# Three product banks instead of four: a streamed half unit of Wo kept in PSUM, and the left K and V half passes placed anew

## The chip, the cores and the metric

The kernel runs on one core of one Trainium2 chip. The metric is the time of one execution on the device in microseconds; a time given for a kernel is the median of several runs.

## The reference

The program computes `x + A(xn) + B(xn)`, where `xn` is the layer norm of `x` (2048 rows of 1024, bf16). `B` is a two-layer perceptron with a GELU (1024 to 3584 to 1024). `A` is a recurrent attention: the rows are cut into 64 segments of 32, and each segment attends to 8 memory rows and itself; the memory rows that come out are the memory of the next segment. So the 64 segments follow one another.

```python
for s in range(n_seg):                      # 64 segments
    xs = x[:, s * seg_len:(s + 1) * seg_len, :].copy()
    h = jnp.concatenate([mem, xs], axis=1)  # 8 + 32 rows
    q = jnp.einsum('btd,dhe->bhte', h, Wq)  # 32 heads of 128
    k = jnp.einsum('btd,dhe->bhte', h, Wk)
    v = jnp.einsum('btd,dhe->bhte', h, Wv)
    scores = jnp.einsum('bhqe,bhke->bhqk', q, k) * scale
    scores = jnp.where(mask[None, None], scores, -1000000000.0)
    p = _softmax(scores, axis=-1)
    o = jnp.einsum('bhqk,bhke->bhqe', p, v)
    o = jnp.einsum('bhte,hed->btd', o, Wo)
    mem = o[:, :M, :].copy()
    outs.append(o[:, M:, :])
```

## The kernel before, in words

**Two stages.** The first stage (up to about 428 us) is the layer norm and the perceptron over all rows. The second is the loop over the 64 segments (line 626), which this change is about.

**Units.** The four weight matrices of the attention are cut into 64 units of 128 partitions x 2048 bf16 (512 KB). Wk, Wq and Wv have 16 each (eight slices of the contraction, times two halves of the heads, u = 0 and 1), Wo has 16, of two heads each. SBUF holds 46 of them for good ("resident"); the other 18 are "streamed": each segment loads them anew from copies in DRAM named `Wc_...` (line 192) into a ring of six slots (`RING`, `STREAM_BUFS`). Two are special. `IN_PSUM`, the fourth of the streamed ones (a unit of Wq), is held in PSUM in two banks named `kept`, and VectorE copies it into its ring slot each segment (line 226). `HALF`, the first streamed unit of Wo, has one of its two heads resident in `half_home`; its other half (256 KB) is streamed.

**Order in a segment.** TensorE works in program order through six half passes and the output product: K0, Q0, K1, Q1, V0, V1 (eight units each), then O (16 units). After each streamed unit `unit_done` calls `start_stream`, which starts the load (SyncE's queue) or the copy (VectorE's queue) of the streamed unit six places further on; nothing else sets the order of the loads. A scheduler doesn't reorder anything: each engine executes its instructions in the order of the source.

**Banks.** A half pass accumulates in one PSUM bank that `new_acc` takes from `free_banks` (four names, `acc0` to `acc3`, in turn), and `let_go` gives it back in program order; a matmul into a bank waits until the copy out of it is done. Of the eight banks four are `acc`, one is `mixed` (scores and softmax sums in its lower half, memory rows and some of the value products in its upper half), one `beside` (masks and kept parts of q), two `kept`. The output product's bank is `psX`.

**Left rows.** Of each segment's 32 rows 24 are worked on with the 8 memory rows, as 32. The 8 rows that are "left" are gathered over a group of four segments (32 rows, `hrL`) and pass through each half pass once a group: a left half pass doubles the products of that half pass. With i4 = 0 to 3 the segment's place in its group (line 627), lines 636 to 639 say where: left K in both half passes at i4 = 0, left Q0 at 1, left Q1 at 2, left V in both at 3. The first segment does all of them. The output product takes the left rows along at i4 = 1. Up to six of a left half pass's products (of resident units) are made ahead of time at the end of the segment before (`lead_products`, line 659), while TensorE would wait for the memory rows; the bank of this left product stays taken until then.

**Attention work inside the passes.** The lists `at` (lines 856 to 892) say after which unit of a pass a step is put: `scores(0)` after Q1's first unit, `sums(0)` after its last; in V1 `scores(1)` after the first unit, `values(0, 0)`, `values(0, 1)`, `sums(1)` after units 2, 4 and 6; in O `values(1, 0)` and `values(1, 1)` after units 4 and 6. `scores(u)` fills `mixed`, ScalarE takes the exponential, VectorE applies the mask (L770). `sums(u)` sums on TensorE, ScalarE takes the logarithm and an exponential for the reciprocal (L788, L789), VectorE multiplies (L790, L792). `values(u, r)` multiplies with v and copies the result to `d_oL` (u = 0) or `b_oL` (u = 1), the inputs of the output product. Rows of K and Q are copied from PSUM by ScalarE (L693) and transposed on VectorE (L707); left ones are copied by VectorE too (`turn_kL`, `turn_qL`), and left V rows by VectorE (`left_values`, L697). `q_left` (L729) puts the left rows of q beside the segment's.

**GpSimd's queue** carries the small loads: the next rows (`load_x_rows`), the next left rows (`load_left_rows`, after K1 of a segment with i4 = 0), the residual rows (`load_res`), and the writes of the output.

Of the kernel before, what the change touches and what calls it, by code (L numbers as in the profile page):

```python
# [78 lines left out]
def kernel(  # L79
# [105 lines left out]
    for k in range(7):  # L185
# [7 lines left out]
        unit: dram.tile([P, 1024 if unit == HALF else 2048], BF16, name="Wc_" + "_".join(map(str, unit)))[:, :]  # L193
        for unit in ORDER if IS_STREAMED[unit]
    }

    def fetch(t, unit):
        w, i, u = unit
        if unit == HALF:
            h = 4 * i + 2 * u  # L200
            nc.sync.dma_start(out=half_home[:, :], in_=Wo_v[:, h, :])
            nc.sync.dma_start(out=t, in_=Wo_v[:, h + 1, :])
        elif w == "O":
            h = 4 * i + 2 * u
            nc.sync.dma_start(out=t.rearrange("p (h d) -> p h d", d=DM), in_=Wo_v[:, h:h + 2, :])
        else:
            nc.sync.dma_start(out=t, in_=W_v[w][:, i, 2048 * u:2048 * u + 2048])
# [12 lines left out]
    def start_stream():  # L220
        nonlocal started
        if started < len(streams):
            t = slab(RING[started % STREAM_BUFS])
            if streams[started] == IN_PSUM and "kept" in nxt:
                for b in range(2):
                    nc.vector.tensor_copy(out=t[:, 1024 * b:1024 * b + 1024], in_=nxt["kept"][:, b, :])  # L226
            else:
                c0 = 1024 if streams[started] == HALF else 0
                nc.sync.dma_start(out=t[:, c0:2048], in_=copies[streams[started]])
# [3 lines left out]
    nxt = {}  # L233
# [37 lines left out]
    with tc.tile_pool(name="ma", bufs=2) as ma, tc.tile_pool(name="mps", bufs=6, space=PSUM) as mps:  # L271
# [160 lines left out]
        for tg in range(4):  # L432
# [80 lines left out]
            else:  # L513


                for _ in range(STREAM_BUFS):
                    start_stream()
                fetch_resident(*(place for place in RES_PLACES if place.startswith("w1_")))
# [29 lines left out]
                fetch_resident("xt2", "xt3")  # L548

# [5 lines left out]
    with tc.tile_pool(name="late", bufs=1) as late, \  # L555
# [7 lines left out]
        free_banks = deque(f"acc{k}" for k in range(4))  # L563
# [12 lines left out]
        tr = mixed[:, 256:512].bitcast(BF16).rearrange("p (c t) -> p c t", c=4)  # L576
# [5 lines left out]
        kept = banks.tile([P, 2, 1024], BF16, name="kept")  # L582

        def keep_unit(t):

            for n in range(4):
                for k in range(4):
                    nc.tensor.transpose(tr[:, k, :], t[:, 512 * n + P * k:512 * n + P * (k + 1)], ident)
                turned = late.tile([P, 512], BF16, name="VL0").rearrange("p (k t) -> p k t", k=4)
                nc.vector.tensor_copy(out=turned, in_=tr)  # L590
                for k in range(4):
                    c0 = 512 * (n % 2) + P * k
                    nc.tensor.transpose(kept[:, n // 2, c0:c0 + P], turned[:, k, :], ident)
            nxt["kept"] = kept
# [29 lines left out]
        for t in outs:  # L624
            nc.vector.memset(t[:, :, 0:32], 0.0)
        for s in range(NSEG):
# [9 lines left out]
            left_k = i4 == 0  # L636
            left_q = [first or (i4 == 1 and more), first or (i4 == 2 and more)]
            left_v = first or (i4 == 3 and more)
# [29 lines left out]
            def half_pass(w, u, left, at):  # L668
# [10 lines left out]
                for i in range(KT):  # L679
# [4 lines left out]
                    if first and (w, i, u) == IN_PSUM:  # L684
                        keep_unit(t)
# [108 lines left out]
            def values(u, r):  # L794

                V, (prA, prB) = st["V", u], st["pr", u]
                low_bank = r == 1 or (left_v and not first)
# [41 lines left out]
            psK, psKL = half_pass("K", 0, left_k, {})  # L839
            turn_k(psK, 0)  # L840
            if left_k:
                turn_kL(psKL, 0)
            psQ, psQL = half_pass("Q", 0, left_q[0], {})
            if first:
                turn_qL(psQL, 0)
# [5 lines left out]
            psK1, psK1L = half_pass("K", 1, left_k, {})  # L851
            st["kT", 1] = nat_home
            rows_out(psK1, nat_home, nc.scalar.copy)
            if left_k and more and not first:
                load_left_rows(g + 1, nc.gpsimd)
# [4 lines left out]
            if left_k:  # L860
                at[1] = [lambda: turn_kL(psK1L, 1)]
            psQ1, psQ1L = half_pass("Q", 1, left_q[1], at)
# [7 lines left out]
            psV, psVL = half_pass("V", 0, left_v, {})  # L870
# [4 lines left out]
            if left_v and not first:  # L875
# [6 lines left out]
            psV1, psV1L = half_pass("V", 1, left_v, at)  # L882
            st["V", 1] = values_out(psV1, sp.tile([P, 512], BF16, name="v", tag="a"), nc.scalar.copy)
            if first:
# [3 lines left out]
            if first:  # L888
# [4 lines left out]
            if left_v and not first:  # L893
# [107 lines left out]
```

## Time and profile before

| what | value |
|---|---|
| median of 7 runs | 1980.27 us (1973.54 to 1989.91) |
| the profiled execution's own time | 1986.99 us |
| its span, first to last instruction | 1985.2 us |
| granted TensorE clock, mean | 0.982 |
| PE busy | 1774.6 us (89%) |
| PEld (weight loads) busy | 963.9 us (49%) |
| DVE busy | 854.7 us (43%) |
| ACT busy | 591.2 us (30%) |
| POOL busy | 287.0 us (14%) |
| DMA moved | 644.36 MB, mean 325 GB/s |

How to read it: PE is TensorE's matmuls, PEld its weight loads, DVE VectorE, ACT ScalarE, POOL GpSimd, SP SyncE, whose queue issues nearly all weight loads. The busy share of PE is not its peak: matmuls overlap, and their ends are modelled. A row of the page's groups names line, engine, operation, what it writes and reads, how often, and then busy time, mean ns of one, and the idle time of its engine ahead of it with the releaser of most of that. "issue" is time for which no releaser is seen. The line numbers are those of the kernel before.

### The profile page before, as it was taken

To read this page: it belongs to the slowest core of one execution; us is meant where nothing else is said; L and a number is where in the kernel's file an instruction comes from. 1 tells how busy PE (TensorE), PEld (TensorE's weight loads), DVE (VectorE), ACT (ScalarE), POOL (GpSimd) and SP (SyncE) were. 2 spreads that over 40 slices of the span, in tenths; PEclk is the share of its full clock that TensorE was granted. 3 is DMA by queue.
4 is the path that set the end of the run, shared out by engine and by line. 5 is a ranking of instruction groups with operands and counts; after the bars stand their busy time and mean duration, and the time that the engine had idled before them with its cause. 6 is when DMAs were issued, how large, how long until landed. Compare 5 with 4: busy or idle time off the path is not lost.

```text
span 1985.2 us, 77130 instructions
## 1 busy us (share of the span) xinstructions
PE 1774.6 (89%) x34271; PEld 963.9 (49%) x34291; DVE 854.7 (43%) x2233; ACT 591.2 (30%) x1349; POOL 287.0 (14%) x557
## 2 busy tenths in 40 slices
PE   6999999999798989898888888889888989889887
PEld 3444444445445554455454545455545455544544
DVE  6656565424343443343434333434344343444333
ACT  4433333312222222232222222222222222222222
POOL 0000000002331111111111111111111111111112
PEclk9999999999999999999999999999999999999999
DMA  9821212789999999999999999999999999999998
GB/s 328 271 52 46 53 44 52 266 304 377 380 356 379 377 382 360 359 385 375 373 373 380 386 363 368 383 364 381 361 388 368 388 377 390 376 382 381 364 354 334
DMA packets 225850, 644.36 MB, mean 325 GB/s; under 512 B 48123, under 2 KB 61739, under 8 KB 225500
## 3 DMA queue, kind: packets, MB, share of 16 engines
q1 hardware_dynamic: 207228, 619.26, 83.2%
q0 software_dynamic: 16928, 18.77, 2.9%
q8 instruction: 268, 4.39, 0.9%
q10 hardware_dynamic: 1360, 1.39, 0.2%
q14 instruction: 66, 0.54, 0.1%
HBM read 625.08 MB, written 31.26 MB: 331 GB/s over the span
## 4 chain that ended last, share of the span: by engine, by line
PE 64%; DMA 25%; issue 6%; DVE 3%; ACT 1%; POOL 1%; ACTq 0%; POOLq 0%; DVEq 0%
PE acc L650 28%; DMA u<-Wc_O 12%; PE acc L829 11%; PE ps L450 10%; DMA u<-Wc_V 9%; PE ps L498 7%; DMA u<-Wc_Q 3%; PE ps L531 2%; DMA out_dram<-res 2%; PE mixed L803 1%; DVE b_oL L707 1%; PE acc L803 1%; PE mixed L753 1%; PE pT L531 1%; DMA res<-hr_d 1%
## 5 line engine op out<-in xcount | busy, mean ns | idle before, releaser
L650 PE MATMUL acc<-u,hr 128*32 128x512 bf16 x11520 | 790.6, 382 | 32.3 <-DMA u<-Wc_V 13.5
L650 PEld LDWEIGHTS <-hr 128*32 128x32 bf16 x12288 | 350.9, 97 | 309.4 <-issue 66.2
L650 PE MATMUL acc<-u,hrL 128*32 128x512 bf16 x2880 | 263.8, 394 | 7.3 <-issue 7.2
L829 PE MATMUL acc<-u,d_oL 128*32 128x256 bf16 (+1 forms) x3330 | 187.0, 294 | 21.9 <-issue 14.1
L450 PE MATMUL ps<-u 128*128 128x512 bf16 x896 | 196.2, 382 | 2.6 <-ACT u L346 2.6
L829 PE MATMUL acc<-u,b_oL 128*32 128x256 bf16 (+1 forms) x1776 | 126.4, 302 | 55.4 <-DMA u<-Wc_O 27.7
L829 PEld LDWEIGHTS <-b_oL 128*32 128x32 bf16 (+1 forms) x3552 | 115.0, 102 | 113.9 <-issue 82.4
L498 PE MATMUL ps<-u 128*128 128x512 bf16 x657 | 146.2, 379 | 0.8
L450 PEld LDWEIGHTS <-u 128*128 128x128 bf16 x896 | 88.2, 98 | 109.3 <-issue 5.1
L829 PEld LDWEIGHTS <-d_oL 128*32 128x32 bf16 (+1 forms) x3552 | 101.4, 99 | 65.7 <-issue 40.0
L650 PEld LDWEIGHTS <-hrL 128*32 128x32 bf16 x3072 | 90.1, 98 | 66.1 <-issue 27.8
L829 PE MATMUL acc<-W_O,b_oL 128*32 128x256 bf16 (+1 forms) x1776 | 111.5, 300 | 7.5 <-issue 7.5
L879 POOL DMA_DIRECT2D res<-hr_d x64 | 35.8, 559 | 567.2 <-DVE d_oL L816 325.6
L707 DVE STREAM_TRANSPOSE kT<-kT 128x512 bf16<-128x512 bf16 x64 | 45.5, 711 | 167.0 <-ACT kT L693 167.0
L226 DVE COPY u<-kept 128x1024 bf16<-128x1024 bf16 x126 | 81.1, 686 | 79.3 <-PE acc L829 62.7
L803 PEld LDWEIGHTS <-v 32*128 32x128 bf16 x2048 | 63.6, 91 | 101.0 <-issue 76.8
L707 DVE STREAM_TRANSPOSE b_oL<-b_oL 128x512 bf16<-128x512 bf16 x128 | 90.6, 708 | 45.9 <-ACT b_oL L693 45.9
L693 ACT CAST kT<-acc 128x512 bf16<-128x512 f32 x64 | 37.4, 585 | 224.4 <-PE acc L650 224.4
L498 PEld LDWEIGHTS <-u 128*128 128x128 bf16 x672 | 65.3, 98 | 77.4 <-DVE g_u L466 0.4
L816 DVE CAST b_oL<-acc 128x160 bf16<-128x160 f32 x128 | 41.5, 324 | 139.9 <-PE acc L809 139.9
L963 POOL DMA_DIRECT2D out_dram<-res x124 | 63.4, 517 | 248.1 <-DVE res L925 247.5
L693 ACT CAST b_oL<-acc 128x512 bf16<-128x512 f32 x128 | 75.4, 589 | 79.5 <-PE acc L650 79.5
(139 smaller groups left out, 2222.5 us busy)
## 6 DMA issues: line engine op xcount, KB each, us to landing
u<-Wc_O SPq DMA_DIRECT2D x320, 512.0 KB
u<-Wc_K SPq DMA_DIRECT2D x256, 512.0 KB
u<-Wc_V SPq DMA_DIRECT2D x256, 512.0 KB
u<-Wc_Q SPq DMA_DIRECT2D x193, 512.0 KB
u<-Wc_O SPq DMA_DIRECT2D x64, 256.0 KB
u<-in_B_w_dram SPq DMA_DIRECT2D x16, 448.0 KB
u<-in_B_w_dram SPq DMA_DIRECT2D x14, 512.0 KB
u<-in_A_Wq_dram SPq DMA_DIRECT2D x12, 512.0 KB
```

The source lines that it names most:

```text
L226: nc.vector.tensor_copy(out=t[:, 1024 * b:1024 * b + 1024], in_=nxt["kept"][:, b, :])
L450: nc.tensor.matmul(ps[:, :].rearrange("p (s t) -> p s t", t=SEG), lhsT=w1_sb[fb // 14 * 8 + kt][:, (fb % 14) * P:(fb % 14 + 1) * P], rhs=x ...
L498: nc.tensor.matmul(ps[:, :], lhsT=gts[fc // 4][:, fc % 4, t * P:(t + 1) * P], rhs=w2_sb[fc // 2][:, fc % 2, cs], start=(fc == 0), stop=(fc ...
L531: nc.tensor.matmul(pss[2 * t + nb][:, :], lhsT=gts[fc // 4][:, fc % 4, t * P:(t + 1) * P], rhs=w2_sb[fc // 2][:, fc % 2, nb * 512:nb * 512 ...
L650: nc.tensor.matmul(o, lhsT=lhs[:, i, :], rhs=m, start=(i == seq[0]), stop=(i == seq[-1]), tile_position=(0, 32 * j),)
L693: cp(out=out, in_=ps.rearrange("p (h e) -> p h e", e=32))
L707: nc.vector.transpose(out=home, in_=home)
L803: nc.tensor.matmul(oV[b][:, c, :], lhsT=V[q, c * P:(c + 1) * P], rhs=prA[q, c, :], start=(c == 0), stop=False, skip_group_check=True, tile ...
L816: cp(out=outs[u][:, hs, NL * slot:NL * slot + 40], in_=oV[b])
L829: nc.tensor.matmul(acc[r:r + n // 8, 0:n], lhsT=lhs[:, 4 * (i % 4) + 2 * u + k, :], rhs=w_k[:, n * jq:n * jq + n], start=(unit == O_UNITS[ ...
L879: nc.gpsimd.dma_start(out=st["res"][:, :], in_=hr_d[s + 1, :, 256:512])
L963: nc.gpsimd.dma_start(out=out_flat[rows, 256 * j:256 * j + 256], in_=res[32 * j:32 * j + NX, :])
```

## The change

Four things change together.

1. `kept` has three banks instead of two, and `free_banks` three names instead of four. The third bank keeps the half of `HALF` that was streamed. `start_stream` copies it from PSUM into its ring slot with one VectorE instruction each segment, in place of a 256 KB load. The slot and its place in the ring stay.
2. `IN_PSUM` and `HALF` have no copy in DRAM any more. The first time `IN_PSUM` is loaded from the weights. `half_home` is loaded once by a DMA of its own, and the other half is loaded into `d_oL` at the end of the first stage, from where it goes to PSUM. `keep` fills a bank by transposing 1024 columns twice on TensorE with copies by VectorE and ScalarE between; `keep_unit` did the same for all 2048 columns with VectorE's copies alone. The zeroing of `d_oL` and `b_oL` moves behind it in the first segment.
3. The left half passes: K0 at i4 = 3 and K1 at i4 = 0 (before: both at 0), V0 at i4 = 3 and V1 at i4 = 0 (before: both at 3). The products made ahead are those of K1, Q0, Q1 and K0 (before: K0, Q0, Q1, V0). The left K0 rows, made at i4 = 3, are turned after Q1's second unit; the left V1 rows are copied at the end of V1. The next left rows are loaded after V1 of a segment with i4 = 0.
4. In `values`, the upper half of `mixed` is used for one of the two results also when the segment has a left V half pass (u = 0), as before for left V segments in both.

```diff
     def start_stream():
...
-            if streams[started] == IN_PSUM and "kept" in nxt:
-                for b in range(2):
-                    nc.vector.tensor_copy(out=t[:, 1024 * b:1024 * b + 1024], in_=nxt["kept"][:, b, :])
+            unit = streams[started]
+            if unit in kept_in:
+                for c0, bank in kept_in[unit]:
+                    nc.vector.tensor_copy(out=t[:, c0:c0 + 1024], in_=bank)
+            elif unit in copies:
+                nc.sync.dma_start(out=t[:, :], in_=copies[unit])
             else:
-                c0 = 1024 if streams[started] == HALF else 0
-                nc.sync.dma_start(out=t[:, c0:2048], in_=copies[streams[started]])
+                fetch(t[:, :], unit)
...
                 for _ in range(STREAM_BUFS):
                     start_stream()
+                h = 4 * HALF[1] + 2 * HALF[2]
+                nc.sync.dma_start(out=half_home[:, :], in_=Wo_v[:, h, :])
...
                 fetch_resident("xt2", "xt3")
+                nc.sync.dma_start(out=d_oL[:, :], in_=Wo_v[:, h + 1, :])
...
-        free_banks = deque(f"acc{k}" for k in range(4))
+        free_banks = deque(f"acc{k}" for k in range(3))
...
-        kept = banks.tile([P, 2, 1024], BF16, name="kept")
-
-        def keep_unit(t):
-
-            for n in range(4):
+        kept = banks.tile([P, 3, 1024], BF16, name="kept")
+
+        def keep(unit, c0, w, bank):
+
+            turned = [late.tile([P, 512], BF16, name=f"VL{n}").rearrange("p (k t) -> p k t", k=4) for n in range(2)]
+            for n in range(2):
                 for k in range(4):
-                    nc.tensor.transpose(tr[:, k, :], t[:, 512 * n + P * k:512 * n + P * (k + 1)], ident)
-                turned = late.tile([P, 512], BF16, name="VL0").rearrange("p (k t) -> p k t", k=4)
-                nc.vector.tensor_copy(out=turned, in_=tr)
+                    nc.tensor.transpose(trs[n][:, k, :], w[:, 512 * n + P * k:512 * n + P * (k + 1)], ident)
+                (nc.scalar.copy if n else nc.vector.tensor_copy)(out=turned[n], in_=trs[n])
+            for n in range(2):
                 for k in range(4):
-                    c0 = 512 * (n % 2) + P * k
-                    nc.tensor.transpose(kept[:, n // 2, c0:c0 + P], turned[:, k, :], ident)
-            nxt["kept"] = kept
+                    c1 = 512 * n + P * k
+                    nc.tensor.transpose(kept[:, bank, c1:c1 + P], turned[n][:, k, :], ident)
+            kept_in.setdefault(unit, []).append((c0, kept[:, bank, :]))
...
-            left_k = i4 == 0
+            left_k = [first or (i4 == 3 and more), i4 == 0]
...
-            left_v = first or (i4 == 3 and more)
+            left_v = [first or (i4 == 3 and more), i4 == 0]
...
-                low_bank = r == 1 or (left_v and not first)
+                low_bank = r == 1 or (u == 0 and left_v != [False, False])
...
             if first:
+                keep(HALF, 1024, d_oL, 2)
+                for t in outs:
+                    nc.vector.memset(t[:, :, 0:32], 0.0)
                 turn_qL(psQL, 0)
...
-            if left_k and more and not first:
-                load_left_rows(g + 1, nc.gpsimd)
...
-            if left_k:
+            if left_k[1]:
                 at[1] = [lambda: turn_kL(psK1L, 1)]
+            elif left_k[0]:
+                at[1] = [lambda: turn_kL(psKL, 0)]
...
-            if first:
+            if left_v[1]:
                 left_values(1, psV1L)
...
-            if first:
+            if i4 == 0 and more:
                 load_left_rows(g + 1, nc.gpsimd)
...
-            if left_v and not first:
-                at[6].append(lambda: left_values(1, psV1L))
...
-                    w, u = (("Q", 0), ("Q", 1), ("V", 0), ("K", 0))[i4]
+                    w, u = (("Q", 0), ("Q", 1), ("K", 0), ("K", 1))[i4]
```

## The prediction

> **What bounds the kernel now.** I read the page first, then the busy time by stretch for one group of four segments, then the chain of waits in that group, the waits of TensorE, and VectorE's timeline. The page (slices of the span, queues, one group row):
>
> ```profile
> DMA  9821212789999999999999999999999999999998
> GB/s 328 271 52 46 53 44 52 266 304 377 380 356 379 377 382 360 359 385 375 373 373 380 386 363 368 383 364 381 361 388 368 388 377 390 376 382 381 364 354 334
> ...
> q1 hardware_dynamic: 207228, 619.26, 83.2%
> ...
> q8 instruction: 268, 4.39, 0.9%
> ...
> L226 DVE COPY u<-kept 128x1024 bf16<-128x1024 bf16 x126 | 81.1, 686 | 79.3 <-PE acc L829 62.7
> ```
>
> From the ninth slice on, the 64 segments run and the DMA digit is 9: the 16 DMA engines have something in hand nearly always. Stretches of four segments (start:end, length, busy time of PE, PEld, DVE, ACT, POOL, granted clock, DMA share, GB/s):
>
> ```profile
> 1026.67:1050.84 24.17, 20.64 (x533) 12.10 (x529) 9.98 (x26) 6.75 (x17) 3.04 (x6) 1.00 1.01 374
> 1050.84:1074.69 23.85, 22.63 (x456) 11.52 (x452) 10.28 (x27) 6.66 (x18) 3.69 (x8) 1.00 1.00 373
> 1074.69:1097.60 22.91, 19.68 (x512) 11.32 (x505) 9.19 (x25) 6.75 (x18) 4.84 (x10) 1.00 1.01 390
> 1097.60:1122.14 24.54, 22.97 (x577) 13.17 (x573) 9.71 (x26) 7.24 (x18) 3.87 (x7) 1.00 1.02 393
> ```
>
> These are segments with i4 = 0, 1, 2, 3 (I call them A, B, C, D). The share is 1.00 and more in each, whatever left work it holds. The chain of waits in the same group (start, length, what):
>
> ```profile
> 1031.79 6.91 DMA u<-Wc_V
> ...
> 1039.19 6.83 DMA u<-Wc_O
> ...
> 1067.04 4.03 PE acc L829 x36
> ...
> 1086.18 7.79 DMA u<-Wc_O
> ```
>
> A transfer takes about 7 us from its release to its landing although 512 KB need 1.4 us at 375 GB/s: it stands in a queue of others. In A and C the chain goes through the O units' weights; in B, whose output product is twice as wide, it stays on TensorE from 1062.5 on. TensorE's own waits from 470 to 1960 us (total, times, longest):
>
> ```profile
> PE acc L829 <- issue: 50.3, 37, 3.3
> PE acc L829 <- DMA u<-Wc_O: 34.2, 62, 1.2
> ...
> PE acc L650 <- DMA u<-Wc_V: 12.6, 26, 1.4
> ```
>
> Waits for weights are spread thin, and mostly lie in V and O. The "issue" waits name no releaser; in the packets of queue q8 most of those over 0.5 us end some 1.4 us after a 16 KB instruction block came in, so I read them as TensorE waiting for instructions. So two things pace it: bytes, and in the dense O phase the instruction blocks.
>
> **What the Trainium skill says.** "DMA: Bandwidth & Descriptors", Specifications, gives about 358 GB/s as the memory's limit per core and 435 GB/s as the ceiling of the fabric. The trace shows 375 on the mean and 393 in one segment, so the first is no hard limit here and the second is near: the bytes are what counts. "VectorE: DVE Perf Modes", "Why PSUM operands drop a tier", lets a bf16 copy from PSUM go at two elements a cycle at best; the row above has 686 ns for 1024, which agrees. "Runtime: NRT & Kernel Launch", Instruction fetch mechanics, says instructions come in 16 KiB blocks over a queue of their own, mostly hidden; the block size agrees (4.39 MB in 268), "hidden" does not, going by the 50.3 us above. "PSUM — Partial Sum Buffer", "PSUM bank collisions raise a hardware error", asks that engines be kept apart by bank and quadrant, so a matmul into a bank waits until its old content is copied out; no wait for an acc bank stands among the large ones of the trace.
>
> **The change part by part.**
> *256 KB less each segment.* The half of unit HALF is no longer loaded. 0.262 MB / 375 GB/s = 0.70 us of all engines; of the 9.0 MB that a segment moves (375 x 24.0 us) it is 2.9%. Over the 62 segments from 470 to 1960 us: at most 43 us. That is the whole prize. It falls at a good place: the load was issued after the fourth unit of Q's second half pass, and the five O units behind it move up. Upper bound for a group: 4 x 0.70 = 2.8 us. In B, where the chain is on TensorE in O, only the V wait can gain: I take off 0.35.
>
> *One VectorE copy more each segment*, 0.69 us, when Q's second half pass has used its fourth unit. In VectorE's queue it stands behind the transpose of K's rows (L857, and the left K turn where there is one), and ahead of the two multiplications of the softmax (L790, L792), the left part of q (L729) and the q transpose (L707), for which scores(1) waits. VectorE in A before:
>
> ```profile
> 1032.97 0.70 DVE L857 STREAM_TRANSPOSE d_oL<-d_oL 128x512 bf16<-128x512 bf16 x1
> 1033.60 0.65 DVE L693 CAST kL<-acc 128x512 bf16<-128x512 f32 x1
> 1034.29 0.71 DVE L707 STREAM_TRANSPOSE kL<-kL 128x512 bf16<-128x512 bf16 x1
> 1034.92 0.28 DVE L790 TENSOR_TENSOR pr<-pr,mixed 128x160 bf16<-128x160 bf16 x1
> ...
> 1035.35 0.70 DVE L707 STREAM_TRANSPOSE b_oL<-b_oL 128x512 bf16<-128x512 bf16 x1
> ```
>
> No gap: in A the copy moves the q transpose by 0.69 us, and scores(1) already waits 0.34 us for it there (before 1036.11). Against it, two left products (0.43 us) come between, as V's second pass now is a left one: +0.35 us. In B VectorE has 0.39 us free before L790: +0.25. In C it idles over 1 us there: nothing. In D the K turn is new (1.36 us), but V's first pass then has eight left products (1.7 us) on TensorE: nothing, and without that cover 0.7.
>
> *Left passes spread anew.* The number stays: 2, 1, 1, 2 half passes a group. A: K0 to V1; D: V1 to K0. The lead products stay six. New in A: VL[1] must be copied (0.68 us) behind the multiplications (0.53 us after the Exp) before values(1, 0), which stands five O units (1.07 us) after V's end; before, that copy came after values(1, 1). I get TensorE waiting 0.7 us; both ends 0.3 and 0.9. The load of the next left rows moves from after K1 to the end of V in A, behind one more load on POOL; a landing takes 5.6 us and the lead that needs it comes 6.6 or more later: nothing, at worst 0.5.
>
> *Three banks.* Half passes use two in turn: pass n+2 needs the bank that ScalarE copies (0.59 us) while pass n+1 runs (1.7 us): nothing. values(u, 1) now takes the bank of values(u, 0), two units before: 0.43 us of TensorE, and the copy is done some 0.5 us after the last matmul: 0.1 us, twice a segment, 0.8 a group; it could be zero or 0.3 each.
>
> Sum of new waits per group: 0.35 + 0.7 + 0.25 + 0.8 = 2.1 us. Most lie just ahead of O, where TensorE waits anyway: in A of this group 0.25, 0.21, 0.85 and 0.66 us for weights. A wait that comes earlier lets transfers and instruction blocks catch up. I take 0.8 as paid, the bounds being 0 and 2.1. Net per group 2.8 - 0.35 - 0.8 = 1.65, per segment 0.41, times 62: **-25.6 us**.
>
> *The first segment.* Filling PSUM before takes from 434.3 to 439.6 us. Now three calls of some 1.8 us each (two sets of transposes, one copy of up to 0.6, two sets) = 5.4, the same; but the third needs d_oL, loaded last on SP, behind the last resident, issued at 436.4 before. With 4 to 7 us to land it is there at 441 to 443: +2 to +3; and both passes of a step on three banks wait for VectorE's copies, some 1.5. I take +4, bounds 0 and 8. The 0.75 MB not copied in DRAM earlier lie under the dense part, where the DMA digit is 1 or 2: nothing.
>
> Total -21.6: from the profiled execution's 1987.0 (span 1985.2) to 1965.4; that execution was 6.7 over the median, so from 1980.3 it is **1959**.
>
> **The rivals.** *Absorbed:* O is paced by instruction blocks, so fewer bytes free only C's waits, 0.70 a group x 15.5 = 11 us, and the first segment and a part of the new waits take 7 back: 1976. For it: the 50.3 us of "issue" in L829, more than the waits for weights. Against it: the DMA share of 1.00 in each segment; a kernel not held by bytes would show less somewhere.
> *Slower:* VectorE's longer queue in Q becomes the pace. Then scores(1) pays the copy in every class and nothing hides it: 2.1 + 0.7 (half of C's and D's copies) = 2.8 a group, 43 us, plus 4 at the start, less some 17 (a third of the 50.7 us that TensorE waits for weights): +30, 2010. It decides from the point where the new waits exceed the 0.70 us a segment that bytes give. For it: the gapless queue in A. Against it: VectorE is busy 43%, and B to D have room.
> That the copy isn't there can't be: the built program has it once a segment in the place told.
>
> **How the numbers follow.** Forecast 0.62 (1938 to 1970), absorbed 0.18, slower 0.20. From 1980.3, 43 us less is 1937, which needs everything hidden. The range 1938 to 2000 leaves about 0.04 below and 0.12 above. A measurement can tell about 0.5% (10 us) from no change: faster 0.62, same 0.18, slower 0.20. Cases of both signs are in it; the likeliest one's own range is 1938 to 1970.
>
> **What would show it.** Right: q1 moves 16 to 18 MB less, GB/s stays at 370 to 380 at share 0.99, segments take 23.4 to 23.7 us, and the waits of L829 for Wc_O fall. Absorbed: share falls to 0.97 and "issue" grows. Slower: the waits of scores(1) (L753) for b_oL grow from 5.5 us to 30 or more, or acc matmuls wait for ScalarE.

## The result, and the profile after

The changed kernel takes 1999.89 us (median of 12 runs, 1990.13 to 2006.7) against 1981.55 us for the kernel before in the same comparison: ratio 1.0097, 95% interval 1.0074 to 1.0119. It is slower by 0.7 to 1.2%, some 19 us more, where 21.6 us less were forecast. Ratios here and below leave out single runs that are over 1.5% above the fastest of the same kernel, which matters for one experiment. The changed kernel's profiled execution has a span of 1998.7 us at a mean granted clock of 0.977. In this section lines have moved: the product is L652 (before L650), O is L832 (L829), scores are L756 (L753), the copy from `kept` is L223 (L226).

The page of the kernel after (slices of the span, two queues, one group row):

```profile
DMA  9821212788989999999999999999999999999998
GB/s 328 246 53 44 54 43 53 287 308 322 365 285 375 368 360 364 361 340 361 374 380 375 370 380 349 372 351 388 354 373 348 378 355 375 346 363 356 352 370 325
...
q1 hardware_dynamic: 197980, 601.96, 81.3%
...
q8 instruction: 268, 4.39, 0.9%
...
L223 DVE COPY u<-kept 128x1024 bf16<-128x1024 bf16 x190 | 122.8, 674 | 83.8 <-PE acc L832 68.0
```

The change does what it says: q1 moves 17.3 MB less (619.26 - 601.96), and VectorE makes 190 copies from PSUM instead of 126. The instruction blocks are the same 268. But the rate fell with the bytes: from 470 to 1960 us the DMA share is 0.97 at 362 GB/s (before: 0.99 at 375). So the engines got idle time, not the kernel. Four segments with i4 = 0 to 3 from the same part of the span as shown of before (start:end, length, busy time of PE, PEld, DVE, ACT, POOL, clock, DMA share, GB/s):

```profile
1040.08:1064.22 24.14, 20.88 (x541) 13.31 (x539) 10.02 (x26) 6.75 (x17) 3.16 (x7) 1.00 0.99 375
1064.22:1087.16 22.94, 22.55 (x456) 11.62 (x452) 10.65 (x28) 6.76 (x18) 3.73 (x8) 1.00 1.02 384
1087.16:1110.33 23.17, 20.51 (x520) 11.95 (x516) 9.77 (x26) 6.66 (x17) 4.83 (x10) 0.93 0.99 379
1110.33:1133.69 23.36, 20.44 (x539) 11.86 (x535) 10.22 (x26) 6.66 (x17) 3.87 (x7) 1.00 0.99 373
```

This group takes 93.6 us, the one shown of before 95.5: one group tells nothing, since a few stalls decide it. Taken from one copy of K's rows (`kT`) to the next, segments 8 to 59 take 24.06 us on the mean after and 23.99 before. The first segment takes 45.0 us instead of 38.3, and segment 4 takes 36.8 instead of 27.8. In these two executions, then, 16 us lie in two segments and 4 in the 52 later ones. Executions of one kernel differ by some 10 us, so such differences of single traces only point to places; the ratios below decide.

TensorE's own waits after, from 470 to 1960 us (total, times, longest):

```profile
PE acc L832 <- issue: 49.3, 32, 3.3
PE acc L832 <- DMA u<-Wc_O: 23.6, 35, 1.6
PE acc L652 <- DMA hrL<-hrL_d: 14.3, 10, 3.8
PE mixed L756 <- DVE b_oL L710: 12.7, 14, 1.2
PE acc L652 <- issue: 11.3, 15, 1.2
PE acc L652 <- DMA u<-Wc_V: 9.1, 17, 1.2
PE acc L652 <- DVE res L929: 9.0, 2, 6.6
...
PE acc L652 <- DVE kL L696: 3.9, 12, 0.3
PE acc L806 <- DVE VL L700: 2.8, 13, 0.2
```

The waits for weights fell (50.7 us for all `Wc_` before, 39.6 after), and so did "issue" (101.3 to 80.5, all lines together). In their place stand a wait for the left rows, which wasn't there at all, and twice the waits for VectorE (17.9 to 35.7). In all TensorE waits 171.0 us in this window, and 171.3 before. The chain of waits in the first of the four segments shows what the left rows' load has become (start, length, what):

```profile
1053.12 0.53 POOL res L885
...
1054.11 0.54 POOL hr L235
...
1054.78 6.03 DMA hrL<-hrL_d
...
1060.86 0.83 PE acc L652 x12
```

GpSimd issues three loads one after the other, the third is the left rows, it takes 6.03 us, and the products made ahead at the end of the segment start on its landing. No weight load is in that stretch of the chain, so fewer bytes of weights could shorten it only through this landing (median of all groups 5.8 us here, and 3.3 us in the run below that halves all streamed loads).

### The profile page after: what moved, and what is told of

Same layout as the page of the kernel before. It is cut to its first block, busy times and chain, and to the rows that moved or that the text cites. A ratio compares the mean times of both kernels' runs of the same rounds, so it can differ in the third digit from the quotient of the medians.

```text
span 1998.7 us, 77198 instructions
## 1 busy us (share of the span) xinstructions
PE 1780.6 (89%) x34287; PEld 975.6 (49%) x34307; DVE 890.1 (45%) x2296; ACT 592.4 (30%) x1352; POOL 287.0 (14%) x557
## 3 DMA queue, kind: packets, MB, share of 16 engines
q1 hardware_dynamic: 197980, 601.96, 81.3%
q8 instruction: 268, 4.39, 0.9%
## 4 chain that ended last, share of the span: by engine, by line
PE 61%; DMA 24%; DVE 6%; issue 5%; ACT 2%; POOL 1%; ACTq 0%; POOLq 0%; DVEq 0%; SPq 0%
PE acc L652 27%; PE acc L832 10%; PE ps L448 10%; DMA u<-Wc_O 8%; PE ps L496 7%; DMA u<-Wc_V 7%; DMA hrL<-hrL_d 3%; DMA out_dram<-res 2%; DMA u<-Wc_Q 2%; PE ps L531 2%; PE mixed L806 1%; DVE b_oL L710 1%; DVE u L223 1%; PE acc L806 1%; DVE d_oL L861 1%
## 5 line engine op out<-in xcount | busy, mean ns | idle before, releaser
L652 PE MATMUL acc<-u,hr 128*32 128x512 bf16 x11520 | 788.8, 383 | 36.0 <-DMA u<-Wc_V 11.1
L652 PEld LDWEIGHTS <-hr 128*32 128x32 bf16 x12288 | 352.3, 97 | 309.4 <-issue 65.5
L652 PE MATMUL acc<-u,hrL 128*32 128x512 bf16 x2880 | 262.1, 396 | 25.0 <-DMA hrL<-hrL_d 14.3
L832 PE MATMUL acc<-u,d_oL 128*32 128x256 bf16 (+1 forms) x3330 | 182.3, 293 | 9.3 <-issue 8.9
L832 PE MATMUL acc<-u,b_oL 128*32 128x256 bf16 (+1 forms) x1776 | 127.9, 307 | 55.7 <-issue 29.3
L832 PEld LDWEIGHTS <-b_oL 128*32 128x32 bf16 (+1 forms) x3552 | 117.4, 105 | 115.0 <-issue 81.7
L223 DVE COPY u<-kept 128x1024 bf16<-128x1024 bf16 x190 | 122.8, 674 | 83.8 <-PE acc L832 68.0
L652 PEld LDWEIGHTS <-hrL 128*32 128x32 bf16 x3072 | 88.9, 99 | 87.4 <-issue 30.4
L832 PE MATMUL acc<-W_O,b_oL 128*32 128x256 bf16 (+1 forms) x1776 | 115.0, 309 | 10.9 <-issue 10.9
L832 PEld LDWEIGHTS <-d_oL 128*32 128x32 bf16 (+1 forms) x3552 | 101.1, 99 | 46.5 <-issue 19.0
L806 PEld LDWEIGHTS <-v 32*128 32x128 bf16 x2048 | 64.7, 91 | 98.1 <-issue 62.7
L700 ACT CAST v<-acc 128x512 bf16<-128x512 f32 x128 | 75.3, 589 | 72.2 <-PE acc L652 72.2
```

The costliest lines, as they stand in the source:

```text
L223: nc.vector.tensor_copy(out=t[:, c0:c0 + 1024], in_=bank)
L652: nc.tensor.matmul(o, lhsT=lhs[:, i, :], rhs=m, start=(i == seq[0]), stop=(i == seq[-1]), tile_position=(0, 32 * j),)
L700: cp(out=t[:, :], in_=ps[:, :])
L806: nc.tensor.matmul(oV[b][:, c, :], lhsT=V[q, c * P:(c + 1) * P], rhs=prA[q, c, :], start=(c == 0), stop=False, skip_group_check=True, tile ...
L832: nc.tensor.matmul(acc[r:r + n // 8, 0:n], lhsT=lhs[:, 4 * (i % 4) + 2 * u + k, :], rhs=w_k[:, n * jq:n * jq + n], start=(unit == O_UNITS[ ...
```

## The experiments

All ratios are to the kernel before on the same chip, with the 95% interval. Waits of TensorE are totals from 470 to 1960 us.

### What the bytes are worth

**The load taken away, its slot kept:**

```diff
-                c0 = 1024 if streams[started] == HALF else 0
-                nc.sync.dma_start(out=t[:, c0:2048], in_=copies[streams[started]])
+                if streams[started] != HALF:
+                    nc.sync.dma_start(out=t[:, :], in_=copies[streams[started]])
...
-                    w_k = half_home if unit == HALF and k == 0 else t[:, 1024 * k:1024 * k + 1024]
+                    w_k = half_home if unit == HALF else t[:, 1024 * k:1024 * k + 1024]
```

> The kernel before with the load of the half unit left out and nothing in its place (part of the computation is changed: both heads of that unit of Wo use the resident half). It prices the bytes alone. Theory 1 (bytes set the pace, full worth 0.70 us a segment): 35 to 45 us faster, 1937 to 1947, ratio 0.977 to 0.982. Theory 2 (TensorE and its instruction blocks set it): 5 to 12 us faster, ratio 0.994 to 0.998.

Measured: 0.9996 (0.9970 to 1.0022), with no copy, no third bank and no new pass in the way. The share fell to 0.97 and the rate to 361 GB/s; waits for weights were 52.0 us (before 50.7), "issue" 100.8 (101.3). The 43 us of the prediction's upper bound are not there.

**The slot taken away as well** (the unit left out of `streams`, its products from `half_home`):

```diff
-    streams = [unit for _ in range(NSEG) for unit in ORDER if IS_STREAMED[unit]]
+    streams = [unit for _ in range(NSEG) for unit in ORDER if IS_STREAMED[unit] and unit != HALF]
```

> The kernel before with the half unit neither loaded nor given a ring slot, so that the six slots serve 17 units instead of 18 (both heads of that unit of Wo use the resident half: part of the computation is changed). The load left out with its slot kept gave nothing (ratio 0.9996). Theory S (slots, not bytes: a load can't be issued before a slot comes free, so what counts is how far ahead the ring reaches): 15 to 35 us faster than before, ratio 0.982 to 0.993. Theory P (TensorE with its instruction blocks and granted clock sets the pace, loads hardly matter): within 8 us of before, ratio 0.996 to 1.002.

Measured: 0.9965 (0.9943 to 0.9988). Waits for weights 27.5 us, "issue" 110.5. With its slot gone too, the six slots serve 17 units and the other loads can start earlier: 7 us in all, a sixth of 43.

**Half of each streamed load** (each streamed unit loads half its columns, used twice):

```diff
-                c0 = 1024 if streams[started] == HALF else 0
-                nc.sync.dma_start(out=t[:, c0:2048], in_=copies[streams[started]])
+                c0, c1 = (1024, 1536) if streams[started] == HALF else (0, 1024)
+                nc.sync.dma_start(out=t[:, c0:c1], in_=copies[streams[started]][:, 0:c1 - c0])
```

> The kernel before with every streamed load half as large (half of the columns, used twice: part of the computation is changed); number of loads, slots and instructions as before. It says what all waiting for weights is worth. Theory P (TensorE sets the pace): TensorE's waits for weights go (some 1.1 us a segment by the trace), and part of this comes back as a lower granted clock: 20 to 60 us faster, ratio 0.97 to 0.99, DMA share about 0.55 to 0.6. Bytes as the bound (the theory of the prediction): segments fall to TensorE's own 20 to 21 us, 180 us or more faster, ratio under 0.91.

Measured: 0.8903 (0.8867 to 0.8938), 20.61 us a segment, at a share of 0.73 and 227 GB/s from 470 to 1700 us. TensorE's waits:

```profile
PE acc L652 <- issue: 12.6, 13, 1.7
...
PE acc L835 <- issue: 3.0, 6, 1.4
```

No wait for weights is left, and "issue" went from 101.3 to 18.3 us in all, with as many instructions a segment: less traffic takes the instruction waits away too. The theory of bytes as the bound foretold this ratio (under 0.91), so the traffic as a whole does hold this kernel; what the runs above deny is that a few bytes of it are worth their share. 4.33 MB a segment less (9.01 to 4.68) gave 3.38 us, 0.78 us for a MB, where the prediction reckoned 2.67 (one over 375 GB/s). In the 20.6 us TensorE hardly waits any more (29.9 us in all from 470 us on, where it was 171.3), so 3.4 us a segment is about all that bytes can win.

**A seventh slot**, with all loads, and **a seventh slot without the half unit's load**:

```diff
-STREAM_BUFS = 6
+STREAM_BUFS = 7
...
         def fetch_late(unit):
+            if unit == RESIDENT[-1]:
+                res_tiles[unit] = res_tiles[RESIDENT[-2]]
+                return
```

> The kernel before with seven ring slots instead of six; the place for the seventh is taken from a resident unit of Wo, which is not held: its products use the weights of the resident unit before it, so that part of the output product is computed with other weights. Loads and bytes per segment are the same. Theory 'loads wait for slots, and what counts is the time from a slot's release to the landing': with one load more ahead, TensorE's waits for weights fall from 1.13 us a segment to about 0.6 and the time by 1 to 2%, 1950 to 1965. Rival 'bytes bound at a DMA share of 0.99': the bytes are the same, so the ratio is within 0.4% of 1.

> As the seven-slot kernel, but the half unit is not loaded (its slot stays in the ring; both heads of that unit use the resident half): the experiment with six slots gave a ratio of 0.9996 for this removal. Theory 'loads wait for slots': with a slot more the freed 0.70 us of the DMA engines can be used by the loads behind; 0.2 to 0.5 us a segment less than the seven-slot kernel, a ratio to it of 0.98 to 0.99. Rival 'the removed bytes are worth nothing wherever the slots are, since instruction blocks and TensorE's own work pace it': same as the seven-slot kernel within 0.3%.

Measured: 0.9993 (0.9966 to 1.0021) and 0.9957 (0.9934 to 0.9981). TensorE's waits with seven slots and all loads:

```profile
PE acc L832 <- issue: 66.8, 42, 2.6
PE acc L653 <- issue: 37.2, 29, 2.9
...
PE acc L832 <- DMA u<-Wc_O: 8.3, 14, 0.9
```

The waits for weights nearly vanish (50.7 to 8.3 us), as the slot theory had it, and the time doesn't move, as the slot theory had not and its rival had: "issue" rises from 101.3 to 136.6. Total waits are 170.1 us against 171.3. Weights that come sooner may make instruction blocks come later, or TensorE, no longer held by weights, may reach the end of its instructions sooner; no run tells these apart. The theory "loads wait for slots" falls as the explanation of the whole. Without the half unit the waits for weights are 3.7 us, "issue" stays at 136.7, and the ratio is 0.36% lower: again 7 us instead of 43.

**The load replaced by the copy, nothing else changed:**

```diff
+                if streams[started] == HALF and "kept" in nxt:
+                    nc.vector.tensor_copy(out=t[:, 1024:2048], in_=nxt["kept"][:, 1, :])
+                elif streams[started] != HALF:
+                    nc.sync.dma_start(out=t[:, :], in_=copies[streams[started]])
```

> The kernel before with one part of the change alone: the half unit's load is replaced by one VectorE copy of a kept bank into the same slot at the same place. Four product banks, left passes and first segment stay as before; the bank copied holds half of the other kept unit, so one head of that unit is multiplied with other weights. Prediction's terms for this part: -0.70 us a segment for the bytes and up to +0.35 for the copy in i4 = 0 and +0.25 in i4 = 1, together about -35 us, 0.982. Theory of the runs so far (freed DMA time at this place is not taken up, copy hidden or nearly so): 1.000 to 1.003. Rival 'the copy holds up VectorE's queue': 1.006 or more, with the waits of scores(1) at 12 us or more instead of 5.5.

Measured: 0.9980 (0.9958 to 1.0002), so 4 us, perhaps none. TensorE's waits:

```profile
PE acc L831 <- issue: 50.6, 38, 2.9
PE acc L831 <- DMA u<-Wc_O: 31.2, 45, 1.4
...
PE mixed L755 <- DVE b_oL L709: 13.9, 15, 1.4
```

The waits of scores(1) rise from 5.5 to 13.9 us: 8.4 us over 15.5 groups, 0.54 a group. In the changed kernel they rise by 7.2 us, 0.46 a group, where the prediction had 0.60 for it. So the copy makes TensorE wait about as was said, and yet this kernel isn't slower: the rival by which the copy sets the pace falls too.

### What the left rows and passes cost

**Both left passes anew, four banks, the half unit loaded**; then **K's alone** and **V's alone**:

```diff
-            left_k = i4 == 0
+            left_k = [first or (i4 == 3 and more), i4 == 0]
...
-            left_v = first or (i4 == 3 and more)
+            left_v = [first or (i4 == 3 and more), i4 == 0]
```

> As the run before it, with the fourth product bank given back: so the kernel before with the new left passes and the new first segment alone. Against the run with three banks it prices the bank: Theory 1 (three banks cost some 0.2 us a segment): 10 to 15 us less than it; theory 2 (the waits for a bank are hidden): within 5 us of it. Against the kernel before it prices the new left passes, 15 to 30 us slower (1.008 to 1.015) if the late left rows are what costs, 0 to 5 us if not.

> Four product banks and the half unit loaded, as in the kernel before; only the left K half passes are placed anew (K0 at i4 = 3, K1 at i4 = 0), both left V passes stay at i4 = 3, the next left rows are loaded after K1 as before. With both spread anew and four banks, the ratio was 1.0048. Theory 'V1 at the end of V costs' (VL[1] late ahead of values(1, 0), as the prediction's 0.7 us in A had it): this kernel stays within 0.2% of before, segments with i4 = 0 at 23.9 us. Rival 'the lead products at the end of i4 = 3 are K1's, so that K0 of the next segment has none and i4 = 3 carries a third left pass': this one carries the cost, ratio 1.004 to 1.008.

> Four product banks and the half unit loaded, as in the kernel before; only the left V half passes are placed anew (V0 at i4 = 3, V1 at i4 = 0), both left K passes stay at i4 = 0, the next left rows are loaded after V1 of i4 = 0 as in the changed kernel. Theory 'V1 at the end of V costs': ratio 1.005 to 1.010, with i4 = 0 about 1 to 2 us longer than before and i4 = 3 some 1 us shorter, as i4 = 0 now carries three left half passes. Rival: the ratio is within 0.2% of 1 and the cost is in K.

("The run before it" in the first of these expectations is the one with three banks and the half unit loaded, further down.) Measured: both 1.0048 (1.0028 to 1.0068), K's 1.0013 (0.9996 to 1.0030), V's 1.0042 (1.0024 to 1.0060). Most of the cost lies with V's. But moving V1 also moves the load of the next left rows, which V1 still reads. So that move was made alone.

**The left rows loaded after V1, on GpSimd's queue** and **on ScalarE's**, in the kernel before:

```diff
-            if left_k and more and not first:
-                load_left_rows(g + 1, nc.gpsimd)
...
-            if first:
+            if i4 == 0 and more:
                 load_left_rows(g + 1, nc.gpsimd)
```

> The kernel before with the load of the next left rows moved from after K1 to after V1 of segments with i4 = 0, on GpSimd's queue, and nothing else. Prediction: nothing, at worst 0.5 us a group. Theory 'it costs once, in segment 4, where the queue still holds the writes of the first stage': segment 4 grows from 28 to some 35 us and the rest stays, ratio 1.003 to 1.005. Rival 'it costs in every group': segments with i4 = 0 or 1 grow by 0.5 us or more, ratio 1.006 or more. Second rival, for which the four-bank pair of runs speaks (the same load on the other queue gave nothing): 1.000 to 1.002.

> The kernel before with the load of the next left rows after V1 as in the changed kernel, but on ScalarE's queue; on GpSimd's queue this move alone gave 1.0039. Theory 'the load is late because it stands behind another on GpSimd's queue': 1.000 to 1.002, TensorE's wait for the left rows 2 us or less instead of 6.8. Rival 'any later place costs': 1.003 to 1.005.

Measured: 1.0039 (1.0022 to 1.0056) and 1.0052 (1.0034 to 1.0070). Moving one 64 KB load a group, with no other edit, gives about all that V's new passes cost. The tile `hrL` in the kernel before: what ended the idle time of TensorE and GpSimd before it, and its landing:

```profile
  PE acc L650: 79.8, 15
...
DMA to landing us min/median/max: 4.5/5.6/6.3
```

and with the load moved, on GpSimd's queue:

```profile
  DMA hrL<-hrL_d: 14.9, 7
...
DMA to landing us min/median/max: 5.3/6.0/7.7
```

Before, the load itself waited at GpSimd for K1's last left product (79.8 us) and nobody waited for the load: it was issued 14.3 us ahead of the first weight load from it, on the mean of 13 groups. Moved, it is issued 6.7 us ahead on the mean (5.9 at the least), with a landing of up to 7.7. On ScalarE's queue it is 7.3 us ahead, TensorE's matmuls wait 3.9 us for it where they waited 6.8 on GpSimd's, and the ratio is no better. So a place this late costs on either queue.

How it costs isn't settled. TensorE's wait for the left rows in the first of these two runs is not spread over the groups:

```profile
PE acc L650 <- DMA hrL<-hrL_d: 6.8, 3, 4.0
```

Three groups of 14 wait, and 4.0 of the 6.8 us are one wait in segment 4, the first segment with the moved load. That segment takes 24.8 to 29.5 us in the seven traces with the load in its old place (the halved loads aside), and 27.3 to 36.8 in the twelve with the load moved, 31.6 on the mean against 27.1. The 52 segments from 8 on show no loss: 23.91 and 23.89 us in these two runs, 23.99 before. The ratio 1.0039 is also what the theory "once, in segment 4" had foretold, and not its rival "in every group", though that segment took 30.5 us here and not 35. Yet the wait can't be the whole of it, as the next pair of runs shows.

**The other queue in the changed kernel, and in its four-bank form:**

```diff
             if i4 == 0 and more:
-                load_left_rows(g + 1, nc.gpsimd)
+                load_left_rows(g + 1, nc.scalar)
```

> The changed kernel with one edit: the next left rows are loaded from ScalarE's queue instead of GpSimd's, at the same place (end of V1 of a segment with i4 = 0). Theory 1 (the moved load lands too late: the trace of the changed kernel has 31 us of idle TensorE and weight load before products with hrL, and segment 4 alone takes 9 us more than before): 15 to 25 us less than the changed kernel, 1975 to 1985, ratio to before 0.998 to 1.002. Theory 2 (the wait only stands where another would stand, the new copy on VectorE is what costs): within 5 us of the changed kernel, 1995 to 2002, ratio 1.007 to 1.011.

> The run with four banks, the half unit streamed and the left passes as in the changed kernel (1.0048), now with the next left rows loaded from ScalarE's queue. If the late left rows are what the new left passes cost: 8 to 10 us less, ratio 0.999 to 1.001, no difference from before. If it is the passes' places themselves (left V1 rows late for values, TensorE's work gathered where loads are short): still 1.003 to 1.006.

Measured: 1.0044 (1.0023 to 1.0065) and 1.0050 (1.0031 to 1.0068). The first looked like a gain of 0.5% over the change, but it rests on 16 of 22 runs, because six are over 1.5% above one unusually short run (1971.3 us). The mean of all 22 is 0.63% above before. The second is no gain over its pair (1.0048), although TensorE's waits for the left rows fell from 20.5 to 2.4 us. These runs were made on different chips. So the load went to ScalarE in segment 4 alone, and the changed kernel and the first of these were run once more, on one chip:

> The changed kernel with the load of the next left rows on ScalarE's queue in segment 4 alone; all other groups keep GpSimd's queue. With ScalarE's queue in all groups the ratio to before was 1.0044, the changed kernel itself 1.0097. Theory 'segment 4 alone': segment 4 falls from 37 to 28 us, ratio 1.004 to 1.006. Rival 'late left rows cost in every group': no more than a fifth of the difference goes, 1.008 to 1.010 with segment 4 at 28 us.

> The changed kernel, unaltered, beside its form with the left rows on ScalarE's queue (next but one label), on one chip: both gave 1.0097 and 1.0044 on different chips. Theory 'late left rows cost in every group' (TensorE waits for them 14.3 us in the changed kernel's trace from 470 to 1960 us against 4.6 with the other queue): 1.008 to 1.011 here, and 0.3 to 0.6% above the other. Rival 'the queue makes no difference, the chips did': within 0.2% of it.

> The changed kernel with the load of the next left rows on ScalarE's queue in every group, unaltered from the experiment that gave 1.0044, now on the same chip as the changed kernel. Theory 'late left rows cost in every group': 1.003 to 1.006. Rival 'the chips made the difference': 1.008 or more.

Measured: 1.0113 (1.0084 to 1.0142); the change again 1.0118 (1.0085 to 1.0152), with ScalarE's queue 1.0085 (1.0057 to 1.0113). Segment 4 stayed long in the first (34.7 us), so GpSimd's queue is not what makes it long. In the trace of the repeated change it was 27.3 us; that execution (1989.18 us) was the shortest of its six (median 1999.1), so it doesn't clear segment 4. On one chip the queue makes 0.33%, and the two intervals overlap; whether it makes anything isn't settled.

### Banks and the copy's place

**The changed kernel with the half unit loaded as before** (its part of `kept` isn't filled in the first segment, the three product banks stay)**, and with the copy later in VectorE's queue** (left rows on ScalarE's queue):

```diff
             elif unit in copies:
-                nc.sync.dma_start(out=t[:, :], in_=copies[unit])
+                nc.sync.dma_start(out=t[:, 1024 if unit == HALF else 0:2048], in_=copies[unit])
```

```diff
+                if unit == HALF:
+                    late_copies.append(copy_kept)
...
             at[5] = [load_res]
+            if late_copies:
+                at[2].append(late_copies.pop())
             psV1, psV1L = half_pass("V", 1, left_v[1], at)
```

> The changed kernel, but the half of HALF is loaded again (256 KB a segment) and not copied from PSUM; the third bank of kept lies idle, three product banks and the new left passes stay. Theory 1 (bytes are worth their 0.70 us a segment, and other parts of the change ate it): 25 to 40 us slower than the changed kernel, 2025 to 2040, ratio 1.022 to 1.03. Theory 2 (bytes are worth little, the copy costs about the same): 1990 to 2005, ratio 1.005 to 1.012.

> The changed kernel with the left rows loaded from ScalarE's queue (1.0044), and the copy of the half unit from PSUM put later in VectorE's queue: after the first value products in V1 instead of after Q1's fourth unit, so that it no longer stands ahead of the softmax multiplications and the q transpose. If the copy's place costs: scores(1) waits 0.4 us less in segments with i4 = 0 and some 0.1 in the others, 5 to 12 us less than the run with the left rows alone, ratio 0.998 to 1.002. If VectorE's queue isn't what costs: within 4 us of it, 1.002 to 1.006.

Measured: 1.0054 (1.0021 to 1.0086), against 1.0048 with four banks: three banks cost 0.06%, give or take 0.4. The later copy gave 1.0073 (1.0052 to 1.0095), no better than the same kernel without that edit (1.0044 and 1.0085), although the waits of scores(1) fell from 14.3 and 13.8 us there to 6.2. And loading the half unit in the changed kernel, without the third filling, is not slower than not loading it (1.0054 against 1.0097).

## Why the prediction was wrong, step by step

**The bytes: the step that failed.** "0.262 MB / 375 GB/s = 0.70 us of all engines ... That is the whole prize." The step from a share of 1.00 to time was wrong. Taken away alone, the load gave 0.9996; with its slot 0.9965; beside a seventh slot 0.36%; with the copy in its place 0.9980. That is 0 to 8 us where the sum had 38 (2.8 - 0.35 a group, times 15.5), and it is most of the 41 us by which the forecast missed. A share of 0.99 said only that there was nearly always a load in hand; in this kernel each freed slot asks for the next load at once. The Trainium skill, "Perfetto Trace Analysis", Identifying the Most-Contended Engine, warns that with 16 engines the occupancy of DMA misleads; the runs agree: 0.99 and 0.97 at the same time of execution. Halving the streamed bytes shows the traffic does matter; but it pays 0.78 us a MB, and the 2.9% at this place less. Why instruction waits don't fall with 3% fewer bytes and nearly vanish with 48% isn't settled: between a share of 0.97 and 0.73 nothing was run, and no run took the same bytes away at another place in the ring.

A part of what the freed bytes gave may have gone into TensorE's clock, which the waits don't show. The granted clock was 0.978 on the mean without the load, 0.977 without load and slot, 0.974 and 0.975 with seven slots, against 0.982 to 0.983 for the kernel before beside them. Among single runs of the kernel before, 0.01 of clock goes with 8 to 15 us, so this is 3 to 13 us, as an estimate from these figures; it was not tried. It doesn't bring the 43 us back: with the copy in place of the load the clock was 0.982, as before, and the gain was 4 us.

**"A wait that comes earlier lets transfers and instruction blocks catch up."** That was right: scores(1) waits 8.4 us longer in the copy experiment and nothing is lost. But the prediction applied it to the new waits only. A wait taken away lets others grow in the same way, as seven slots show (weights 42 us less, "issue" 35 more).

**The left rows.** "A landing takes 5.6 us and the lead that needs it comes 6.6 or more later: nothing, at worst 0.5." The load was moved from 14.3 us of room to 6.0 (mean of 13 groups after, 4.9 at the least) with landings up to 6.8. So a median landing was set against a room that turned out smaller, and the term was entered as nothing. The move alone costs 0.39% (7.7 us). Spread over 15.5 groups that is the "worst" of 0.5 us, but the traces don't show it so spread; where it lies is open.

**The left passes.** The 0.7 us for VL[1] in A was too much: L806 waits for VL 13 times, 0.2 us each. The times named for it leave only 0.14 us (0.53 + 0.68 - 1.07). In the same way the 0.35 us for the copy in A should be 0.26 (0.69 - 0.43). Neither decides anything. The left K turn in D, put at nothing, shows as 12 waits of 0.3 us at L652 for `kL`. Both are small; K's passes alone measure 0.13% and include zero.

**Three banks.** 0.8 us a group was entered among the 2.1 us of new waits, of which 0.8 were then taken as paid; 0.06% (1 us, give or take 8) was measured. One longer wait belongs here as a reading only: L652 waits 6.6 us for `res` (L929), the addition that frees the bank of the output product, at the start of segment 4.

**The first segment.** +4 was taken, 0 to 8; the trace has +6.7. Six traces of kernels with the third filling have 42.5 to 45.3 us, those without it 35.6 to 39.8 (the halved loads aside). The waits in it, after:

```profile
PE mixed L592 <- DVE VL L593: 1.7, 3, 0.6
PE acc L652 <- DVE qL_last L696: 1.6, 1, 1.6
PE acc L652 <- DMA hrL<-hrL_d: 1.3, 1, 1.3
PE mixed L592 <- DMA d_oL<-in_A_Wo_dram: 1.2, 1, 1.2
PE kept L597 <- ACT VL L593: 1.2, 3, 0.5
```

and before:

```profile
PE kept L593 <- DVE VL L590: 2.1, 4, 0.5
```

The wait for d_oL is 1.2 us instead of 2 to 3, and those for the copies are 2.9 us against 2.1 before, 0.8 more instead of some 1.5; not foreseen were the left part of q behind the third filling (1.6) and the next left rows (1.3).

**The sum.** Copy in place of the load -4 us (0 to -8), left passes with their rows +9.5 (6 to 13), three banks +1 (-7 to 9), first segment +6.7: +13, against 19 (15 to 24) and 23 (17 to 30) measured. The rest of 6 to 10 us is within what these intervals leave open; it has no place of its own. TensorE's waits for VectorE (17.9 before; 22.5 with the copy alone, 25.4 with the passes alone, 35.7 with all) may point to the two meeting, but kernels with neither have 13.8 to 23.8 us in their traces (the halved loads aside); it is not shown.

**The rivals.** "Absorbed" had the share right (0.97), and its 11 us are nearer to what the bytes alone were worth than the forecast's 38; but "issue" fell in the changed kernel where it should grow, and the time didn't stay. "Slower" had the right side by the wrong mechanism: scores(1) waits 12.7 us, not 30, and the copy alone makes nothing slower.

## What to carry to other kernels

A DMA share near 1 over a ring of buffers says that the ring is kept full, not that bytes set the pace: take away the very bytes that a change would save, without the rest of the change, before pricing them. Here the bandwidth promised 43 us, the slope from halving all loads some 13 (0.78 us a MB, 0.262 MB, 62 segments), and the runs gave 0 to 8. When one kind of wait is taken away from an engine that several things starve, look at what the others do before entering a gain. A small load that is moved later must be priced by its longest landing against the least room, with its place in its queue; and one should look where in the program its waits fall, since they need not repeat with the loop.

## What the runs showed of the hardware

The clock of TensorE was granted at half rate in single stretches, most of 3.4 us and some of 6.8: 17 times in the loop before (61 us), 20 times after (82 us), 25 times with seven slots, once with the halved loads. Of these, 16 of the 17 before and all 20 after begin in a gap of TensorE of over 0.6 us or within about 2 us of its end. There are 112 such gaps in the loop before, and 15 with the halved loads; the gaps and the 2 us behind them are less than a quarter of the loop before. So a stall may cost twice, which was read from the traces and not tried. The Trainium skill, "TensorE: Matmul & The Clock Gate", HAM oscillation — how this bites in real kernels, gives as a rule that idle gaps over about 3.4 us are to be avoided; here, in the kernel before, gaps of 0.6 to 3.3 us went ahead of such stretches. The other surprise is above: queue q8's instruction blocks are 4.39 MB of 627, and TensorE's "issue" waits (80.5 us) are longer than those for the weights (39.6). That they are waits for these blocks is a reading of the packets: of the 73 longer than 0.5 us before, every one ends 1.0 to 1.8 us after a block has come in.
